# First batch of an attention and mixer kernel: token mixer by head pairs and column halves, one PSUM tile over four banks, reordered loads

## The chip, the cores and the metric

The kernel runs on one core of one Trainium2 chip. The metric is the device time of one execution in microseconds (us). Before the change the median was 291.68 us of three timed runs (291.28 to 292.91). Lower is better. Differences under 2% count as the same.

The engines are called PE (TensorE, matmuls), ACT (ScalarE), DVE (VectorE), POOL (GpSimd) and SP (SyncE, which issues stores). PSUM is the memory that PE's matmuls write and that ACT and DVE read here; the kernel divides it into eight banks of 512 fp32 columns.

## The reference, cut to what matters

```python
# 8 batches, 8 heads, 576 tokens, head size 64
scores = q @ k^T / 8 + min(-(cum_i - cum_j), 0), causal
attn   = exp(scores - max) / (sum + 1e-9)
x = (attn @ v) laid out as [batch, 576, 512]
h = relu(x^T @ w_tok1) @ w_tok2          # token mixer, 576 -> 256 -> 576
u = x + h^T
out = u + relu(u @ w_ch1) @ w_ch2        # channel mixer, 512 -> 1536 -> 512
```

## The kernel before

The kernel doesn't leave the order to a compiler. It lists operations with estimated durations, a small list scheduler (the plan) puts them in order on each engine, and the kernel then issues them in that order. A `Buf` is a claim on one slot of a ring of buffers. The plan gives it the slot that has been free longest.

All PSUM is in two rings: `psc`, two tiles of two banks each, for scores, and `pmx`, four tiles of one bank each, for nearly everything else:

```python
r_sc = ring("psc", 2, [128, 2, 512], FP32, psum)
r_mx = ring("pmx", 4, [128, 512], FP32, psum)
```

The groups of matmuls that write `pmx` are 316 in all (so many claims the plan makes on its slots): attention times v, token mixer and both channel matmuls of all eight batches. A group is written by PE and read by ACT or DVE, and with four slots PE can run up to three groups ahead of the readers. The tile framework adds the semaphores that keep a write and a read of the same tile apart.

The first channel matmul is the pattern that fills most of the time:

```python
pm = Buf(r_mx, False)
...
def mm(cc=cc, pm=pm, a=a, e=e):
    for m in range(NMC):          # 4 matmuls into one bank
        nc.tensor.matmul(out=pm.t[:, 0 : e - a], lhsT=wc1[:, m, bass.ds(cc * 128, 128)],
                         rhs=uT.t[:, m, a:e], start=(m == 0), stop=(m == NMC - 1))
...                               # then relu of that bank into g, on ACT or DVE
```

In batch one, scores of two head pairs go to two `pmx` slots (`Duo`) where `psc` is short. The causal mask is either a DVE multiplication behind the exponential, or, for the blocks in the list `FOLD`, matmuls that add -30000 to the scores (a "mask matmul" with the identity as weights):

```python
FOLD = ((0, 0), (0, 1), (1, 0), (1, 1), (2, 1), (3, 1))   # (head pair, group)
```

Where the plan sees PE idle in the first 95 us, the kernel puts matmuls on a zero tile there ("filler"), to keep PE's clock up.

## Time and profile before

| | span, profiled | PE busy | DVE | ACT | clock granted to PE |
|---|---|---|---|---|---|
| before | 294.8 us | 282.3 us (96%) | 192.9 us | 169.0 us | 0.981 |

The span is that of the profiled execution, which was a slow one (296.72 us; its clock fell to a half early on, as the prediction reads from it). Busy time counts an engine's instructions. The granted clock is the share of full speed at which PE could run, averaged over the span. The prediction below shows the lines behind this table.

### The profile page before, as it was taken

To read this page: it belongs to the slowest core of one execution; us is meant where nothing else is said; L and a number is where in the kernel's file an instruction comes from. 1 tells how busy PE (TensorE), PEld (TensorE's weight loads), DVE (VectorE), ACT (ScalarE), POOL (GpSimd) and SP (SyncE) were. 2 spreads that over 40 slices of the span, in tenths; PEclk is the share of its full clock that TensorE was granted. 3 is DMA by queue.
4 is the path that set the end of the run, shared out by engine and by line. 5 is a ranking of instruction groups with operands and counts; after the bars stand their busy time and mean duration, and the time that the engine had idled before them with its cause. 6 is when DMAs were issued, how large, how long until landed. Compare 5 with 4: busy or idle time off the path is not lost.

```text
span 294.8 us, 6480 instructions
## 1 busy us (share of the span) xinstructions
PE 282.3 (96%) x2565; PEld 161.9 (55%) x2597; DVE 192.9 (65%) x427; ACT 169.0 (57%) x286; POOL 45.3 (15%) x97
## 2 busy tenths in 40 slices
PE   7799999999999999999899999999999999999993
PEld 3348875656764554546664544536764454447642
DVE  7746947899998988999976687897236350530022
ACT  4365775989977858537781239672860346108500
POOL 8674600121111012102100022100000000000000
PEclk9759999999999999999999999999999999999999
DMA  7999999899674899857941786853002410250032
GB/s 134 222 203 263 216 209 218 183 235 272 95 141 92 116 235 204 163 118 191 170 69 37 143 167 107 123 120 115 0 3 54 129 69 0 58 140 36 3 107 76
DMA packets 58483, 38.60 MB, mean 131 GB/s; under 512 B 44496, under 2 KB 48208, under 8 KB 58448
## 3 DMA queue, kind: packets, MB, share of 16 engines
q0 software_dynamic: 10128, 17.93, 34.9%
q1 hardware_dynamic: 48320, 20.21, 28.4%
q8 instruction: 21, 0.34, 0.5%
q14 instruction: 14, 0.11, 0.1%
HBM read 40.71 MB, written 9.44 MB: 170 GB/s over the span
## 4 chain that ended last, share of the span: by engine, by line
PE 77%; DMA 5%; DVE 3%; issue 2%; ACT 2%; POOL 0%; POOLq 0%; ACTq 0%
PE pmx L979 30%; PE pmx L952 26%; PE psc L670 4%; PE pmx L813 4%; PE pmx L743 4%; PE pmx L883 4%; DMA qkn<-in_q_dram 3%; DMA qkn<-in_k_dram 2%; PE pmx L1098 1%; DVE x L753 1%; ACT junk L598 1%; PE psc L813 1%; DVE vp L570 1%; PE pmx L872 1%; ACT E L698 1%
## 5 line engine op out<-in xcount | busy, mean ns | idle before, releaser
L698 ACT ACTIVATE E<-psc 128x1024 bf16<-128x1024 f32 x62 | 60.3, 1021 | 41.9 <-PE psc L670 36.0
L952 PEld LDWEIGHTS <-wc 128*128 128x128 bf16 x624 | 59.7, 98 | 33.2 <-issue 2.3
L952 PE MATMUL pmx<-uTb,wc 128*128 128x320 bf16 x384 | 54.7, 299 | 1.0 <-ACT gb L959 1.0
L979 PE MATMUL pmx<-wc,gb 128*128 128x512 bf16 (+1 forms) x243 | 54.2, 369 | 0.6 <-issue 0.2
L959 ACT ACTIVATE gb<-pmx 128x320 bf16<-128x320 f32 x73 | 31.0, 440 | 27.2 <-PE pmx L952 22.7
L598 ACT ACTIVATE junk<-qkn 128x1152 bf16<-128x1152 bf16 x32 | 37.2, 1162 | 13.5 <-DMA qkn<-in_k_dram 8.0
L979 PE MATMUL pmx<-wc,ga 128*128 128x512 bf16 x182 | 44.1, 379 | 0.5
L952 PE MATMUL pmx<-uTa,wc 128*128 128x512 bf16 (+1 forms) x235 | 43.1, 336 | 0.4
L979 PEld LDWEIGHTS <-gb 128*128 128x128 bf16 x252 | 23.8, 98 | 24.9 <-issue 0.4
L959 ACT ACTIVATE ga<-pmx 128x512 bf16<-128x512 f32 (+1 forms) x48 | 23.7, 503 | 12.8 <-PE pmx L952 11.7
L706 DVE TENSOR_TENSOR E<-E,keep 128x512 bf16<-128x512 bf16 x58 | 23.9, 415 | 8.1 <-ACT E L698 7.4
L979 PEld LDWEIGHTS <-ga 128*128 128x128 bf16 x192 | 17.7, 98 | 19.7 <-issue 1.0
L753 DVE TENSOR_TENSOR x<-pmx,rc 128x320 bf16<-128x320 f32 x60 | 27.5, 481 | 0.7
L670 PE MATMUL psc<-qT,kT 32*128 32x256 bf16 (+2 forms) x620 | 24.3, 258 | 2.9 <-DVE qT L642 1.9
L570 DVE TENSOR_TENSOR vp<-vf,wT 128x512 bf16<-128x512 f32 (+1 forms) x40 | 26.1, 681 | 1.0 <-DMA vf<-in_v_dram 0.8
L743 PEld LDWEIGHTS <-E 128*128 128x128 bf16 x576 | 21.5, 97 | 6.4 <-issue 0.9
L670 PEld LDWEIGHTS <-kT 32*128 32x128 bf16 x640 | 15.3, 95 | 16.7 <-issue 14.4
L743 PE MATMUL pmx<-vp,E 128*128 128x65 bf16 x540 | 21.8, 193 | 0.0
L991 DVE TENSOR_TENSOR of<-pmx,ub 128x512 f32<-128x512 f32 (+1 forms) x17 | 11.2, 658 | 15.7 <-PE pmx L979 15.4
L642 DVE STREAM_TRANSPOSE qT<-qkn 128x576 f32<-128x576 f32 x16 | 19.9, 1241 | 2.3 <-DMA qkn<-in_q_dram 2.3
L991 DVE TENSOR_TENSOR of<-pmx,ua 128x512 f32<-128x512 f32 x12 | 8.3, 691 | 19.5 <-PE pmx L979 17.5
L592 POOL DMA_DIRECT2D qkn<-in_k_dram x20 | 10.8, 542 | 65.3 <-DVE E L714 36.9
(98 smaller groups left out, 245.5 us busy)
## 6 DMA issues: line engine op xcount, KB each, us to landing
out_dram<-of SPq DMA_DIRECT2D x31, 256.0 KB, 2.3
vf<-in_v_dram SPq DMA_DIRECT2D x24, 256.0 KB, 6.3
qkn<-in_k_dram POOLq DMA_DIRECT2D x20, 288.0 KB, 5.6
qkn<-in_q_dram POOLq DMA_DIRECT2D x20, 288.0 KB, 6.4
vf<-in_v_dram POOLq DMA_DIRECT2D x8, 256.0 KB, 9.1
wc<-in_moe_w_ch_dram POOLq DMA_DIRECT2D x4, 384.0 KB, 8.1
wc<-in_moe_w_ch_dram POOLq DMA_DIRECT2D x3, 512.0 KB, 11.5
out_dram<-of SPq DMA_DIRECT2D x10, 128.0 KB, 2.4
```

Source lines behind the costliest of these rows:

```text
L570: eng.tensor_tensor(out=vp.t[p0 : p0 + n, c, :, 0:D], in0=vf.t[p0 : p0 + n, c, :, :], in1=wT[p0 : p0 + n, cw, b * H : b * H + H].unsqueeze ...
L598: P.op({"ACT": (1.2, 1.6, lambda: nc.scalar.activation(out=junk[:, :], in_=n.t[:, :], func=AF.Square, accum_out=sq[:, col : col + 1]))}, r ...
L642: P.op({"DVE": (1.24, 1.4, lambda n=n, dst=dst: nc.vector.transpose(out=dst.t[:, 0:S, :].rearrange("d t e -> d (t e)").bitcast(FP32).rearr ...
L670: nc.tensor.matmul(out=pss[g // 2].bank(g % 2)[:, o], lhsT=kT.t[rows, j0 : j0 + 128, e], rhs=qT.t[rows, a:z, e], start=(e == 0 and not (fo ...
L698: nc.scalar.activation(out=E.t[:, :, gi * 512 : gi * 512 + 512], in_=ps.t[:, :, :], func=AF.Exp, scale=0.125)
L706: nc.vector.tensor_tensor(out=o, in0=o, in1=keep[:, :].unsqueeze(1).unsqueeze(1).to_broadcast([128, 2, 2, 128]), op=ALU.mult)
L743: nc.tensor.matmul(out=o[:, i, ic, 0 : D + 1], lhsT=E.t[:, hh, d0 : d0 + 128], rhs=vp.t[:, jc, h + hh, 0 : D + 1], start=(jc == j_lo), sto ...
L753: nc.vector.tensor_tensor(out=x.t[:, :, h0 * D : (h0 + n) * D].rearrange("p c (e d) -> p e c d", e=n), in0=view()[:, :, :, 0:D], in1=rc.t[ ...
L952: nc.tensor.matmul(out=pm.t[:, 0 : e - a], lhsT=wc1[:, m, bass.ds(cc * 128, 128)], rhs=uT.t[:, m, a:e], start=(m == 0), stop=(m == NMC - 1))
L959: lambda cc=cc, pm=pm, a=a, e=e: nc.scalar.activation(out=g.t[:, cc, a:e], in_=pm.t[:, 0 : e - a], func=AF.Relu),
L979: nc.tensor.matmul(out=pm.t[:, 0 : d1 - d0], lhsT=g.t[:, cc, c * 128 : c * 128 + 128], rhs=wc2[:, cc, d0:d1], start=(cc == 0), stop=(cc == ...
L991: nc.vector.tensor_tensor(out=o.t[:, d0:d1], in0=pm.t[:, 0 : d1 - d0], in1=src.t[:, si, d0:d1], op=ALU.add)
```

## The change

The intent is to shorten the way from the first scores to the first channel matmul, and to close holes in PE's order behind it. The core of the diff, cut:

```diff
-    LAG = 3.0
+    LAG = 2.5
-    FOLD = ((0, 0), (0, 1), (1, 0), (1, 1), (2, 1), (3, 1))
+    FOLD = ((0, 1), (1, 0), (1, 1), (2, 0), (2, 1), (3, 0), (3, 1))
...
-    r_mx = ring("pmx", 4, [128, 512], FP32, psum)
+    banks = psum.tile([128, 4, 512], FP32, name="pmx", tag="pmx")
+    r_mx = Ring("pmx", [banks[:, i, :] for i in range(4)])
...  (class Duo: two slots are now one access over two banks)
+        def t(self):
+            lo, hi = sorted(x.slot for x in self.bufs)
+            return banks[:, lo : hi + 1 : hi - lo, :]
...  (pads: memsets on DVE become copies of a zero tile on ACT)
...  (normalisation: by pairs, the third pair as ten copies with a scale on ACT)
-        for hs in ([(0, 1)] if b == 0 and np_ > 1 else [(0,), (1,)]):
+        for hs in ([(0, 1)] if b == 0 else [(0,), (1,)]):
...  (token mixer of batch one: four cuts of two heads, second matmul by column halves)
-        cuts = [[(0, 4)], [(4, 6)], [(6, H)]] if b == 0 else ...
+        cuts = [[(0, 2)], [(2, 4)], [(4, 6)], [(6, H)]] if b == 0 else ...
...  (loads of batch two: keys earlier, second half of the first channel weight later,
...   first part of the second channel weight ahead of the last query; estimates of three loads)
-                 ...], ("wc2", g), 3.1)
+                 ...], ("wc2", g), 2.6)
...  (some of the last stores split in two; a fallback that doesn't run loads through POOL)
```

More of the change, by code (lines that the diff above doesn't have):

```diff
@@ L238, in general @@
             tc.tile_pool(name="genp", bufs=1, space=bass.MemoryType.PSUM) as pp:
-        nc.sync.dma_start(out=scr[:, :], in_=cum[:, :])
+        nc.gpsimd.dma_start(out=scr[:, :], in_=cum[:, :])
         past = gp.tile([128, 1152], FP32, name="gk", tag="gk")
@@ L251, in general @@
                     sl = src[bass.ds(b, 1), bass.ds(h, 1), :, :]
-                    nc.sync.dma_start(out=f[:, 0:4, :],
+                    nc.gpsimd.dma_start(out=f[:, 0:4, :],
                                       in_=sl[:, :, 0:512, :].rearrange("o u (c p) d -> p (o u c) d", p=128))
-                    nc.sync.dma_start(out=f[0:64, 4, :], in_=sl[:, :, 512:576, :].rearrange("o u p d -> (o u p) d"))
+                    nc.gpsimd.dma_start(out=f[0:64, 4, :], in_=sl[:, :, 512:576, :].rearrange("o u p d -> (o u p) d"))
                     n = g2.tile([128, NJ, D], BF16, name="gn", tag=f"gn{len(nat)}")
@@ L267, in general @@
                 nc.vector.memset(cb[:, S:640], 0.0)
-                nc.sync.dma_start(out=cb[:, 0:S], in_=scr[bass.ds(b * H + h, 1), :].to_broadcast([128, S]))
+                nc.gpsimd.dma_start(out=cb[:, 0:S], in_=scr[bass.ds(b * H + h, 1), :].to_broadcast([128, S]))
                 with tc.For_i(0, NJ, 1) as ic:
@@ L339, in general @@
                 nc.vector.tensor_tensor(out=o[:, :], in0=pm[0:64, :], in1=o[:, :], op=ALU.add)
-                nc.sync.dma_start(out=out[bass.ds(b, 1), bass.ds(c * 64, 64), :].rearrange("o p d -> (o p) d"), in_=o[:, :])
+                nc.gpsimd.dma_start(out=out[bass.ds(b, 1), bass.ds(c * 64, 64), :].rearrange("o p d -> (o p) d"), in_=o[:, :])
 @with_exitstack
@@ L478, in late_pads, with ones, tok_pads, v_pads @@
     def late_pads():
-        for i in range(2, 4):
-            P.op({"DVE": (0.15, 0.3, lambda i=i: pads(nc.vector, i)), "POOL": (0.4, 0.6, lambda i=i: pads(nc.gpsimd, i))},
-                 reads=["wT"], writes=[("pad", i)], prio=40)
-        P.op({"DVE": (0.6, 0.8, lambda: pads2(nc.vector)), "POOL": (1.0, 1.2, lambda: pads2(nc.gpsimd))},
-             reads=["wT"], writes=["padw"], prio=41)
-        P.op({"DVE": (0.3, 0.5, lambda: pads3(nc.vector, 1)), "POOL": (0.5, 0.7, lambda: pads3(nc.gpsimd, 1))},
-             reads=["wT"], writes=["padv"], prio=42)
+        def ones(i):
+            nc.scalar.activation(out=r_E.tiles[i][:, :, EW - 64 : EW], in_=zero[:, 0:128].rearrange("p (h n) -> p h n", h=2),
+                                 func=AF.Copy, bias=1.0, scale=1.0)
+        def tok_pads():
+            nc.scalar.copy(out=w1[64:128, NJ - 1, :], in_=zero[64:128, 0:DT])
+            nc.scalar.copy(out=w1[0:64, NJ, :], in_=zero[0:64, 0:DT])
+            nc.scalar.copy(out=w2[:, :, S : NJ * 128], in_=zero[:, 0 : NTC * 64].rearrange("p (t n) -> p t n", t=NTC))
+        def v_pads():
+            for h in range(0, H, 4):
+                nc.scalar.copy(out=r_vp[1].tiles[0][0:64, NJ - 1, h : h + 4, :],
+                               in_=zero[0:64, 0 : 4 * (D + 2)].rearrange("p (h n) -> p h n", h=4))
+        for i in range(2, 4):
+            P.op({"ACT": (0.3, 0.5, lambda i=i: ones(i))}, writes=[("pad", i)], prio=40)
+        P.op({"ACT": (0.9, 1.1, tok_pads)}, writes=["padw"], prio=41)
+        P.op({"ACT": (0.7, 0.9, v_pads)}, writes=["padv"], prio=42)
     s_sb = sb("s_sb", [64, S], FP32, fast)
@@ L545 @@
     vbuf = {}
+    later = []
     gate = sb("gate", [1, 32], BF16, fast)
@@ L561, in stage_v @@
             else:
-                load_p(load, [(vf, c)], (0.75 if b or c <= 1 else 1.25) * n / 128, 1.4)
+                load_p(load, [(vf, c)], (0.75 if b or c == 0 else 1.3) * n / 128, 1.4)
                 yield
@@ L572, in mul @@
                     in1=wT[p0 : p0 + n, cw, b * H : b * H + H].unsqueeze(2).to_broadcast([n, H, D]), op=ALU.mult)
-            P.op({"DVE": (0.72, 0.95, lambda mul=mul: mul(nc.vector))}, reads=[(vf, c), "wT"], writes=[(vp, c)], prio=b * 10 + 5 if b else 0)
+            o = P.op({"DVE": (0.72, 0.95, lambda mul=mul: mul(nc.vector))}, reads=[(vf, c), "wT"], writes=[(vp, c)], prio=b * 10 + 5 if b else 0)
+            if b == 1:
+                later.append(o)
         def ones():
@@ L593, in load_quad @@
             out=n.t[:, :], in_=src[b, 4 * qd : 4 * qd + 4, :, :].rearrange("g (p r) d -> (g p) (r d)", r=R)),
-            [(n, 0)], 128 * 0.19 / 16)
+            [(n, 0)], 128 * 0.182 / 16)
         return n
@@ L620, in __init__ @@
             self.keys = [(x, 0) for x in self.bufs]
+        @property
+        def t(self):
+            lo, hi = sorted(x.slot for x in self.bufs)
+            return banks[:, lo : hi + 1 : hi - lo, :]
         def bank(self, g):
-            return self.bufs[g].t[:, :]
+            return self.t[:, g, :]
     class Solo:
@@ L677, in quad @@
                     fold = (np_ + e, gi) in FOLD
-                    occ = 0.8 + 0.4 * gi if fold else 0.58
+                    occ = 0.6 + 0.1 * gi if fold else 0.55
                     P.op({"PE": (occ, occ + 0.3, lambda e=e, mm=mm, fold=fold: mm((2 * e, 2 * e + 1), fold))},
@@ L691, in soft @@
         odd = b % 2
-        def ex2():
-            for g in range(2):
-                nc.scalar.activation(out=E.t[:, g, gi * 512 : gi * 512 + 512], in_=ps.bank(g), func=AF.Exp, scale=0.125)
         def ex():
             nc.scalar.activation(out=E.t[:, :, gi * 512 : gi * 512 + 512], in_=ps.t[:, :, :], func=AF.Exp, scale=0.125)
-        P.op({"ACT": (1.18, 1.4, ex2)} if isinstance(ps, Duo) else act(1024, ex), reads=ps.keys, writes=[(E, jc) for (jc, a, z) in group], prio=0)
+        P.op(act(1024, ex), reads=ps.keys, writes=[(E, jc) for (jc, a, z) in group], prio=0)
         if b == 0 and (np_, gi) in FOLD:
@@ L726, in pair @@
         vkeys = [(vp, c) for c in range(NJ)] + [(vp, "w")] + (["padv"] if b == 1 else [])
-        for hs in ([(0, 1)] if b == 0 and np_ > 1 else [(0,), (1,)]):
-            pa = Solo(r_sc if b == 0 and np_ > 1 else r_mx)
+        for hs in ([(0, 1)] if b == 0 else [(0,), (1,)]):
+            pa = Duo() if b == 0 and np_ < 2 else Solo(r_sc if b == 0 else r_mx)
             rc = Buf(r_rc, False)
@@ L755, in nrm, with nrm_act @@
                     in1=rc.t[:, 0:n, :].unsqueeze(3).to_broadcast([128, n, NJ, D]), op=ALU.mult)
-            P.op({"DVE": (0.16 + 0.33 * n, 0.38 + 0.33 * n, nrm)}, reads=pa.keys + [(rc, 0)], writes=[(x, h + hh) for hh in hs], prio=0)
+            def nrm_act(view=view, rc=rc, h0=h + hs[0]):
+                for i in range(2):
+                    for c in range(NJ):
+                        nc.scalar.activation(out=x.t[:, c, (h0 + i) * D : (h0 + i + 1) * D], in_=view()[:, i, c, 0:D],
+                                             func=AF.Copy, scale=rc.t[:, i, c : c + 1])
+            P.op({"ACT": (1.5, 1.72, nrm_act)} if np_ == 2 else {"DVE": (0.16 + 0.33 * n, 0.38 + 0.33 * n, nrm)}, reads=pa.keys + [(rc, 0)], writes=[(x, h + hh) for hh in hs], prio=0)
     def load_w(dmas, key, us):
@@ L779, in load_ch2 @@
         load_w([(wc2[:, 4 * g : 4 * g + 4, :],
-                 moe_w_ch2[g * 512 : (g + 1) * 512, :].rearrange("(c p) n -> p c n", p=128))], ("wc2", g), 3.1)
+                 moe_w_ch2[g * 512 : (g + 1) * 512, :].rearrange("(c p) n -> p c n", p=128))], ("wc2", g), 2.6)
     hbuf = {}
@@ L796, in tok @@
         us = Buf(r_us) if odd else None
-        cuts = [[(0, 4)], [(4, 6)], [(6, H)]] if b == 0 else [[(0, 4)], [(4, H)]] if b == 1 else [[(0, H)]]
+        cuts = [[(0, 2)], [(2, 4)], [(4, 6)], [(6, H)]] if b == 0 else [[(0, 4)], [(4, H)]] if b == 1 else [[(0, H)]]
         for part in cuts:
             h0, h9 = part[0][0], part[-1][1]
-            late = h0 > 0
+            late = h0 >= 4
             if late:
@@ L834, in tok, with mmT @@
                 hk = [(h1, t, part[0][0]) for part in cuts if part[0][0] <= 2 * m < part[-1][1] for t in range(NTC)]
-                def mmT(m=m, pm=pm):
-                    o = slice(m * 128, m * 128 + 128)
-                    for t in range(NTC):
-                        nc.tensor.matmul(out=pm.t[:, :], lhsT=h1.t[:, t, o], rhs=w2[:, t, 0:NQ], start=(t == 0), stop=False)
-                    for c in range(NJ - 1):
-                        nc.tensor.matmul(out=pm.t[:, c * 128 : c * 128 + 128], lhsT=x.t[:, c, o], rhs=ident[:, :],
-                                         start=False, stop=(c == NJ - 2))
-                occ = 2 * c_pe(NQ)[0] + 4 * c_pe(128)[0]
-                P.op({"PE": (occ, occ + 0.3, mmT)}, reads=hk + ["w2", (x, 2 * m), (x, 2 * m + 1)],
-                     writes=[(pm, 0)], holds=[uT], prio=(rank - TOK, 1 + 0.1 * m))
-                for a in (0, NQ // 2):
+                for a in (0, NQ // 2):
+                    def mmT(m=m, pm=pm, a=a):
+                        o = slice(m * 128, m * 128 + 128)
+                        for t in range(NTC):
+                            nc.tensor.matmul(out=pm.t[:, a : a + NQ // 2], lhsT=h1.t[:, t, o], rhs=w2[:, t, a : a + NQ // 2],
+                                             start=(t == 0), stop=False)
+                        for c in range(a // 128, a // 128 + 2):
+                            nc.tensor.matmul(out=pm.t[:, c * 128 : c * 128 + 128], lhsT=x.t[:, c, o], rhs=ident[:, :],
+                                             start=False, stop=(c == a // 128 + 1))
+                    occ = 2 * c_pe(NQ // 2)[0] + 2 * c_pe(128)[0]
+                    P.op({"PE": (occ, occ + 0.3, mmT)}, reads=hk + ["w2", (x, 2 * m), (x, 2 * m + 1)],
+                         writes=[(pm, a)], holds=[uT], prio=(rank - TOK, 1 + 0.1 * m + (0.25 if a else 0)))
                     def evT(eng, m=m, pm=pm, a=a):
@@ L852, in evT @@
                             nc.vector.tensor_copy(out=o, in_=i)
-                    P.op(either(NQ // 2, lambda evT=evT: evT(0), lambda evT=evT: evT(1)), reads=[(pm, 0)],
-                         writes=[(uT, m, a)], prio=0)
+                    o = P.op(either(NQ // 2, lambda evT=evT: evT(0), lambda evT=evT: evT(1)), reads=[(pm, a)],
+                             writes=[(uT, m, a)], prio=0)
+            for w in later:
+                w.deps.add(o)
         hkeys = [(h1, t, part[0][0]) for part in cuts for t in range(NTC)]
@@ L1000, in st @@
                     if c < NJ - 1:
-                        nc.sync.dma_start(out=out[b, c * 128 : c * 128 + 128, d0:d1], in_=o.t[:, d0:d1])
+                        parts = 2 if (b == B - 1 and c < 3) or (b == B - 2 and c == 3) else 1
+                        for i in range(parts):
+                            w = (d1 - d0) // parts
+                            f0 = d0 + i * w
+                            nc.sync.dma_start(out=out[b, c * 128 : c * 128 + 128, f0 : f0 + w], in_=o.t[:, f0 : f0 + w])
                     else:
@@ L1020 @@
     load_tok()
+    sv = stage_v(1)
     load_ch1(0, 0)
     load_ch1(0, 1)
-    sv = stage_v(1)
-    for m2 in range(2):
-        next(sv)
-        load_ch1(1, m2)
-    for i in range(2):
-        next(sv)
-        stage_qk(1, 0, (i,))
-    run(sv)
-    stage_qk(1, 1)
-    for g in range(3):
-        load_ch2(g)
+    next(sv)
+    load_ch1(1, 0)
+    next(sv)
+    stage_qk(1, 0, (0,))
+    next(sv)
+    load_ch1(1, 1)
+    stage_qk(1, 0, (1,))
+    next(sv)
+    next(sv)
+    run(sv)
+    stage_qk(1, 1, (0,))
+    load_ch2(0)
+    stage_qk(1, 1, (1,))
+    load_ch2(1)
+    load_ch2(2)
     last[0] = P.op({"SP": (0.6, 0, lambda: nc.sync.dma_start(out=gate[0:1, 16:32], in_=wc2[0:1, NCC - 1, 0:16]))},
```

## The prediction

> **What bounds the kernel now.** I read the page's busy shares and its 40 slices first, then sums over chosen stretches, then the timeline of TensorE (PE), then that of VectorE (DVE) where PE waited, then the waits and the landings of the weight loads.
>
> ```profile
> PE 282.3 (96%) x2565; PEld 161.9 (55%) x2597; DVE 192.9 (65%) x427; ACT 169.0 (57%) x286; POOL 45.3 (15%) x97
> ...
> PEclk9759999999999999999999999999999999999999
> DMA  7999999899674899857941786853002410250032
> ```
>
> PE is busy 96% of a span of 294.8 us; no other engine passes 65%. Adding up its idle time, I find 1.3 us at the start, 0.6 and 1.9 us before the first scores, 1.0 us near 147, 0.5 us near 194 and 4.6 us behind the last matmul (a store and the closing of the program). The rest are crumbs. So the kernel is bound by PE, and a change gains only where PE is idle, slow, or busy with nothing. The second line says slow: the granted clock falls to about a half in slices 2 and 3.
>
> ```profile
> core 0: us, PE busy (x) PEld busy (x) DVE busy (x) ACT busy (x) POOL busy (x), PEclk, DMA share, GB/s
> 10.80:21.00 10.20, 9.84 (x82) 4.27 (x81) 6.47 (x13) 6.43 (x9) 7.59 (x11) 0.50 1.17 198
> 40.20:44.40 4.20, 4.15 (x47) 2.67 (x48) 3.28 (x7) 3.21 (x4) 0.28 (x1) 1.00 1.17 212
> ```
>
> From 10.8 to 21.0 us, which is the scores of the first batch, PE had half its clock: 10.2 x 0.5 = 5.1 us of capacity lost. The DMA share is above 1: the loads of batches one and two and of all weights fill the queues from about 5 to 54 us. The profiled execution took 296.72 us, the timed ones 291.28 to 292.91; the 5.0 us between 296.72 and the median of 291.68 is about this loss. I conclude (it isn't shown) that the timed runs mostly keep the clock in this stage.
>
> "Busy with nothing" is line 1098: matmuls on a zero tile that the schedule puts wherever it believes PE idle, to hold the clock. They count as busy but are holes of the plan. In the timeline of PE (start, length, line, operation, count, idle time before):
>
> ```profile
> 10.29 0.40 PE L670 MATMUL psc<-qT,kT 32*128 32x256 bf16 x4 [1.89 <-DVE qT L642]
> ...
> 23.56 0.55 PE L1098 MATMUL pmx<-zero 128*128 128x512 bf16 x2
> ...
> 24.70 0.25 PE L1098 MATMUL pmx<-zero 128*128 128x205 bf16 x1
> ...
> 29.62 0.81 PE L1098 MATMUL pmx<-zero 128*128 128x512 bf16 x3
> 30.26 0.60 PE L952 MATMUL pmx<-uTa,wc 128*128 128x256 bf16 x4
> ...
> 41.42 1.10 PE L1098 MATMUL pmx<-zero 128*128 128x512 bf16 x4
> 42.45 0.64 PE L670 MATMUL psc<-qT,kT 32*128 32x256 bf16 x24
> 43.02 1.36 PE L1098 MATMUL pmx<-zero 128*128 128x512 bf16 x6
> 44.21 1.89 PE L979 MATMUL pmx<-wc,ga 128*128 128x512 bf16 x8
> ```
>
> Two holes matter. **Hole A**, in the token mixer of batch one: 0.43 us (23.56), 0.24 us (24.70) and 0.65 us (29.62 to 30.3, counting the part that doesn't overlap), about 1.3 us. **Hole B**, ahead of the second channel matmul: from the last L952 at 41.58 to L979 at 44.38 on the chain is 2.80 us with one real piece of 0.57 us in it, so 2.2 us.
>
> What makes hole A is VectorE:
>
> ```profile
> 22.64 0.49 DVE L753 TENSOR_TENSOR x<-pmx,rc 128x320 bf16<-128x320 f32 x1
> ...
> 23.32 1.25 DVE L753 TENSOR_TENSOR x<-pmx,rc 128x320 bf16<-128x320 f32 x3
> 24.49 0.47 DVE L749 RECIPROCAL rc<-psc 128x10 f32<-128x10 f32 x2
> 24.88 1.49 DVE L753 TENSOR_TENSOR x<-psc,rc 128x640 bf16<-128x640 f32 x2
> ```
>
> Normalisation holds DVE from 22.41 to 26.37 without a break, and the first token matmul (24.79) takes four heads at once, so it waits until 24.57, while PE had finished those heads' attention at 23.2. What makes hole B isn't a semaphore: the list of waits has none for PE there. The three loads of the second channel weight were issued at 28.70, 29.54 and 30.88. The first and the last took:
>
> ```profile
> DMA to landing us min/median/max: 9.8/9.8/9.8
> ...
> DMA to landing us min/median/max: 13.8/13.8/13.8
> ```
>
> They landed at 38.5, 41.0 and 44.7, but the plan charges 3.1 us each and so expects them later. In the profiled run hole B was in the plan's estimates more than in the data. The lines of waits have one more thing:
>
> ```profile
> DVE uTa L852 <- ACT uTa L850: 2.4, 3, 1.3
> ```
>
> The two halves of one evacuated bank go to ScalarE and VectorE, and the second engine waits for the first.
>
> **What the Trainium skill says.** "TensorE: Matmul & The Clock Gate", Part 1: the array's clock is halved after a window of some 3.4 us with little activity and restored after a busy one, and the windows run free of the kernel. The trace agrees: 10.2 us at 0.50, three such windows, behind an idle 1.89 us. "PSUM — Partial Sum Buffer", PSUM bank collisions: two engines must be kept apart on one bank. The 2.4 us above is that separation. "VectorE: DVE Perf Modes", Why PSUM operands drop a tier: fp32 from PSUM stays at the base rate, so pairing saves only fixed cost. The trace agrees: 320 columns take 0.48 us, 640 take 1.49/2 = 0.75 us.
>
> **The change part by part.**
>
> Pads to ScalarE: takes two E pads (0.31 us at 10.20), three weight pads (0.45 us) and one v pad (0.28 us) from DVE, 1.04 us. ScalarE was idle from 7.52 to 11.81. Only the 0.31 us stands between two transposes, and the last query lands at 12.54, hence little: 0 to 0.2 us.
>
> Masks: one block of masks leaves PE (pair 0, first group), two come (pairs 2 and 3). A block is four matmuls of 128 columns, 0.05 us each at full clock: +0.2 us of PE, +0.4 at half. The first exponential starts 0.2 to 0.4 us earlier in return. Net 0.
>
> Exponentials over joined banks: two of 512 took 1.09 us, one of 1024 takes 1.02; two places, -0.14 us.
>
> Normalisation: before, DVE took 4 x 0.48 + 4 x 0.16 + 1.49 + 0.47 = 4.5 us by single durations (4.0 us in the timeline, where they overlap). After, three pairs at about 0.95 are 2.9 us, and the fourth pair is ten copies of 64 columns on ScalarE. Its 128-column relu pairs took 0.45 us, 0.22 each, so ten are 1.3 to 2 us (estimate), beside DVE. DVE is free about 1.1 us earlier.
>
> Token mixer by pairs and halves: the same columns on PE (the first two cuts become 20 x 0.056 in place of 10 x 0.108), but the first cut starts after one pair, and the first-half channel matmuls can start while PE still has second halves to do. This fills hole A: I count 1.1 of its 1.3 us.
>
> Loads and estimates: the first second-channel load passes one 288 KB query load, 1.39 us by the landings (34.52 to 35.91), so it lands near 37.1. The estimate falls from 3.1 to 2.6 us, close to the measured 2.55. The filler of hole B should go, but the third load still lands near 44, so some waiting comes back: I count 1.5 of 2.2 us.
>
> The later order (LAG 2.5), the delayed multiplication of v of batch two and the split stores: no sure sign, 0. The last store's chain, issue at 290.67 and landing at 292.85, isn't shortened. The fallback's loads don't run.
>
> Sum: 0.1 + 0.1 + 1.1 + 1.5 = 2.8 us. With a little more for the lower LAG, chosen rather than derived, 3.1 us: 291.7 - 3.1 = 288.6.
>
> **The rivals.** (1) The loads take hole B's place. In a run at full clock PE is up to 5 us earlier, near 36.5 at the end of L952, where the first weight load (37.1) and above all the third (44) bind. For it: DMA share 1.17. Against: scores and attention of batch two are there to fill. Time 290.5. (2) VectorE becomes the bound in batches two and three, where it is busy 9.19 of 10 us (50 to 60) and 18.73 of 20 (60 to 80), and returns the gain. For it: those shares. Against: PE never waits on it there. Time 290 to 291. (3) One joined tile for four banks makes waits between unrelated banks, or ScalarE's ten copies delay the relus behind them: 291.5 to 293. The trace of before can't tell. (4) Both holes close wholly and the warmer PE keeps its clock in more runs: 3.7 us, perhaps 5, thus 286.5 to 288.
>
> **Range and chances.** The gain I can point to is at most 3.7 us of holes plus small change, 1.3%; over 2% (under 285.85) needs a clock effect on top: 0.10. Slower by 2% (above 297.5) needs rival 3 at its worst: 0.02. The range 286.2 to 291.2 spans rivals 1, 2 and 4.
>
> **What would show it.** Right: L952 starts a good microsecond earlier at equal clock; filler between 23 and 30 us and between L952 and L979 nearly gone; DVE's normalisation near 3 us; the first second-channel load landing ahead of a query; the PE timeline behind 60 us shifted, not changed. Wrong: new PE waits on second-channel loads or on DVE between 36 and 60 us; more idle PE behind 100 us than the 1.0 and 0.5; a clock at half for longer or shorter than 10.2 us, which alone moves the time by 1.7 us a window.

## More of the kernel before

One more line, to be held against the changed kernel later, is the sum over 100 us in the steady part (columns: stretch, its length, busy time of PE, weight loads, DVE, ACT and POOL with instruction counts, clock, DMA share, GB/s):

```profile
100.00:200.00 100.00, 97.57 (x918) 52.30 (x928) 83.30 (x186) 61.01 (x96) 11.19 (x29) 1.00 0.72 142
```

PE works 97.6 of 100 us, at full clock.

## The result, and the profile after

The changed kernel took 569.36 us (median of four runs, 565.47 to 574.37) against 291.48 us of the kernel before in the same rounds. The ratio is 1.948, with a 95% interval of 1.931 to 1.966. Ratios here and below are the mean time of one kernel's fast runs over that of the other's of the same rounds, so not quite the ratio of the medians. The output is correct. The profiled run is a fast one; the slow run (574.37 us) counts in the median of four but not in the ratio.

The page of the changed kernel, the lines that answer to those of before:

```profile
span 570.2 us, 6541 instructions
...
PE 376.5 (66%) x2589; PEld 182.9 (32%) x2620; DVE 196.4 (34%) x413; ACT 175.5 (31%) x305; POOL 44.8 (8%) x97
...
PEclk9975997985789999995579979686579999788579
```

No engine is the bound any more. DVE and ACT have nearly the work of before (DVE 196.4 against 192.9 us, ACT 175.5 against 169.0) and PE has the same instructions within 1%, yet PE is busy for 376.5 instead of 282.3 us and idle for 193.7 instead of 12.5 us. Of the 275.4 us by which the span grew, 181.2 us are PE idle and 94.2 us are PE busy for longer. The clock is not lost once, at the start, but again and again over the whole span (mean 0.841). Weighing each busy stretch of PE with the clock granted in it, 66.0 us of its busy time are lost to the clock, against 4.9 us before (an estimate from the two traces). The rest of the 94.2 us is paid at full clock: the four matmuls of the group at 33.60 us, alone but at full clock, took 0.60 us, against the 0.44 us that such four take back to back.

The profile of before is a slow one. Between the fast profiles of the two controls below the split is the same: the span grows by 277.6 us, of which 180.9 us are PE idle and 96.7 us PE busy for longer.

The sums over a stretch early and over the same 100 us as before (same columns):

```profile
40.00:60.00 20.00, 13.91 (x60) 7.34 (x60) 0.00 (x0) 4.60 (x12) 0.00 (x0) 0.62 0.78 153
100.00:200.00 100.00, 62.46 (x518) 31.63 (x523) 46.31 (x101) 36.53 (x58) 6.94 (x21) 0.86 0.39 76
```

From 40 to 60 us all that the compute engines do is 60 matmuls, their weight loads and 12 ACT instructions. Between 100 and 200 us PE issues 518 matmuls instead of 918. This is long behind the first batch, for which the change was written.

What such a stretch is made of is seen in the timelines of PE and ACT (start, length, line, operation, count, idle time before and what ended it):

```profile
39.10 1.01 PE L977 MATMUL pmx<-uTa,wc 128*128 128x256 bf16 x4 [0.47 <-ACT ga L984]
40.59 1.01 PE L977 MATMUL pmx<-uTa,wc 128*128 128x256 bf16 x4 [0.47 <-ACT ga L984]
```

```profile
38.67 0.38 ACT L984 ACTIVATE ga<-pmx 128x256 bf16<-128x256 f32 x1 [1.10 <-PE pmx L977]
40.15 0.38 ACT L984 ACTIVATE ga<-pmx 128x256 bf16<-128x256 f32 x1 [1.10 <-PE pmx L977]
```

The two engines take turns. PE writes a group (39.10 to 40.11), ACT reads (40.15 to 40.53), PE writes the next (from 40.59), with a period of 1.49 us. In the kernel before, the same four matmuls took 0.44 us each time (84 of them in 9.17 us on the chain), and the readers ran beside them. Inside a group the matmuls start 0.21 us apart in place of 0.11: this is half clock (0.50 granted from 39.0 to 41.1 us). The Trainium skill, "TensorE: Matmul & The Clock Gate", A second HAM failure mode: psum-queue depth-cycling, describes PE idling briefly and often between groups until the clock swings between its two states. This trace agrees: 0.47 us idle in each 1.49, and a clock of 0.62 from 40 to 60 us.

The waits of the whole span, the lines that matter (who waited for whom: total us, times, longest):

```profile
ACT gb L984 <- PE pmx L977: 97.8, 55, 25.7
...
PE pmx L977 <- ACT gb L984: 33.1, 55, 1.1
...
PE pmx L977 <- ACT ga L984: 23.0, 33, 1.9
```

The list of before has a single wait of PE for ACT at that line, of 1.0 us. The waits of 33.1 and 23.0 us are the largest that joined the list; waits of PE for DVE, up to 11.4 us in all at a line, joined it too.

With the changed kernel in hand I read the semaphores in the compiled programs, which needs no chip. A group of the first channel matmul in the changed kernel, with the counts that it waits for and reaches:

```
PE   4 matmuls into bank 2   first waits for ACT count 101 (a read of bank 0); last makes PE count 786
ACT  read of bank 1          waits for PE count 786 (the write of bank 2);     makes ACT count 102
PE   4 matmuls into bank 3   first waits for ACT count 102 (the read of bank 1)
```

Every line here waits for another bank than its own. Here each access waits for the last access by another engine to the tile, whatever bank that touched. In the kernel before each bank is a tile, so the same rule makes a group wait for the reader of its own bank, four groups ago. I counted over each program the PE waits whose releaser touches PSUM:

```
                        reader of the same bank   reader of another bank, same tile
kernel before                    305                          3
changed kernel                    31                        277
```

A second count, which puts the wait of a weight load down to the matmul behind it, gave 307 and 1, and 34 and 274.

This makes a theory: the one tile over four banks costs everything (theory A). Three rivals stand against it. In B, the new plan's order, the copies on ACT or the loads lose the time. In C, an instruction that reads two banks is slow. In the third, the loss comes from the banks and their ports, and sharing a tile is incidental.

### The profile page after: what moved, and what is told of

It reads as the page before. It is cut to its first block, busy times and chain, and to the rows that moved or that the text cites. A ratio compares the mean times of both kernels' runs of the same rounds, so it can differ in the third digit from the quotient of the medians.

```text
span 570.2 us, 6541 instructions
## 1 busy us (share of the span) xinstructions
PE 376.5 (66%) x2589; PEld 182.9 (32%) x2620; DVE 196.4 (34%) x413; ACT 175.5 (31%) x305; POOL 44.8 (8%) x97
## 4 chain that ended last, share of the span: by engine, by line
PE 61%; DVE 18%; ACT 12%; issue 6%; DMA 2%; another core or an unknown queue 1%; POOL 0%; DVEq 0%; ACTq 0%; POOLq 0%
PE pmx L977 26%; PE pmx L1004 19%; ACT gb L984 6%; DVE x L768 5%; ACT ga L984 4%; PE pmx L758 4%; DVE of L1016 4%; PE pmx L834 4%; PE pmx L908 2%; DVE gb L986 2%; PE psc L689 2%; DVE rc L764 1%; DVE ub L930 1%; DVE ua L930 1%; DVE ga L986 1%
## 5 line engine op out<-in xcount | busy, mean ns | idle before, releaser
L977 PE MATMUL pmx<-uTb,wc 128*128 128x320 bf16 x384 | 90.4, 379 | 51.1 <-ACT gb L984 33.1
L977 PEld LDWEIGHTS <-wc 128*128 128x128 bf16 x624 | 70.4, 113 | 155.8 <-issue 118.3
L1004 PE MATMUL pmx<-wc,gb 128*128 128x512 bf16 (+1 forms) x243 | 65.1, 405 | 28.3 <-DVE of L1016 7.3
L977 PE MATMUL pmx<-uTa,wc 128*128 128x512 bf16 (+1 forms) x234 | 58.0, 381 | 33.9 <-ACT ga L984 23.0
L1004 PE MATMUL pmx<-wc,ga 128*128 128x512 bf16 x182 | 54.2, 431 | 22.2 <-DVE ub L930 5.1
L768 DVE TENSOR_TENSOR x<-pmx,rc 128x320 bf16<-128x320 f32 (+1 forms) x58 | 28.3, 496 | 30.1 <-PE pmx L1004 8.4
L612 ACT ACTIVATE junk<-qkn 128x1152 bf16<-128x1152 bf16 x32 | 37.1, 1160 | 2.3 <-DMA qkn<-in_k_dram 2.0
L986 DVE TENSOR_SCALAR gb<-pmx 128x320 bf16<-128x320 f32 x21 | 10.3, 491 | 58.3 <-PE pmx L977 40.6
L834 PE MATMUL pmx<-x,w 128*128 128x512 bf16 (+2 forms) x88 | 21.1, 372 | 12.3 <-DVE x L768 4.2
L908 PE MATMUL pmx<-h,w 128*128 128x512 bf16 x55 | 16.2, 387 | 10.9 <-DVE of L1016 4.1
L689 PE MATMUL psc<-qT,kT 32*128 32x256 bf16 (+1 forms) x620 | 22.7, 258 | 0.7
```

What stands on the lines that cost most here:

```text
L612: P.op({"ACT": (1.2, 1.6, lambda: nc.scalar.activation(out=junk[:, :], in_=n.t[:, :], func=AF.Square, accum_out=sq[:, col : col + 1]))}, r ...
L689: nc.tensor.matmul(out=pss[g // 2].bank(g % 2)[:, o], lhsT=kT.t[rows, j0 : j0 + 128, e], rhs=qT.t[rows, a:z, e], start=(e == 0 and not (fo ...
L768: nc.vector.tensor_tensor(out=x.t[:, :, h0 * D : (h0 + n) * D].rearrange("p c (e d) -> p e c d", e=n), in0=view()[:, :, :, 0:D], in1=rc.t[ ...
L834: nc.tensor.matmul(out=pm()[:, (ha - h0) * D : (hb - h0) * D], lhsT=w1[:, NJ if odd and c == NJ - 1 else c, t * 128 : t * 128 + 128], rhs= ...
L908: nc.tensor.matmul(out=pm.t[:, :], lhsT=w2[:, t, c * 128 : c * 128 + 128], rhs=h1.t[:, t, :], start=(t == 0), stop=(t == NTC - 1 and not f ...
L986: lambda cc=cc, pm=pm, a=a, e=e: nc.vector.tensor_scalar_max(out=g.t[:, cc, a:e], in0=pm.t[:, 0 : e - a], scalar1=0.0)),
```

## The experiments

All kernels below leave out the conditional fallback block behind the main part, which never runs with these inputs; it contains a form of weight load that these experiments had to avoid. So two controls come first. The twelve runs gave correct outputs. They were timed in three groups, each on a chip of its own and beside the kernel before (c1, c2, e1, e2; e3 to e6; e7 to e10). Across groups the ratios to the kernel before are compared, rather than the medians.

### The two controls

> Control: the kernel before without the conditional fallback block, which never runs with these inputs (the experiments all leave it out). Every theory: the time of before less at most 1 us of closing, 290 to 292 us; ratio to before 0.995 to 1.00.

> Control: the changed kernel without the fallback block. Every theory: about the time of the changed kernel, 560 to 575 us. If the moved fallback loads were to blame, it would fall to about 290 us; I don't expect that.

The control of before took 290.61 us, ratio 0.995 (0.988 to 1.002). The control of after took 568.06 and 577.05 us, the second slow. The fallback isn't involved.

The control of before had its profile in the fast state (clock 0.998, span 288.7 us), which before's own profile had not. So its timeline shows what the prediction could only infer:

```profile
13.41 0.29 PE L670 MATMUL psc<-qT,kT 32*128 32x256 bf16 x2
...
14.09 0.59 PE L660 MATMUL psc<-negm,ident 128*128 128x512 bf16 x2
...
17.28 1.02 PE L743 MATMUL pmx<-vp,E 128*128 128x65 bf16 x28 [0.48 <-DVE vp L570]
...
25.47 9.33 PE L952 MATMUL pmx<-uTa,wc 128*128 128x256 bf16 x84
...
38.23 1.36 PE L1098 MATMUL pmx<-zero 128*128 128x512 bf16 x6
39.42 1.89 PE L979 MATMUL pmx<-wc,ga 128*128 128x512 bf16 x8
```

The first channel matmul starts at 25.47 us here and the second at 39.42, with filler ahead of it. Both are 4.8 us earlier than in the profile at half clock. The first three lines are for later: from 13.41 to 14.09 us PE does 16 score matmuls, of two head pairs at once, and at 17.28 us attention times v goes on after a wait for v.

### Only the joined tile undone, and only the joined tile done

```diff
 # e1, against the changed kernel
-    banks = psum.tile([128, 4, 512], FP32, name="pmx", tag="pmx")
-    r_mx = Ring("pmx", [banks[:, i, :] for i in range(4)])
+    r_mx = ring("pmx", 4, [128, 512], FP32, psum)
 # and two instructions, one for each bank, where one read both
```

```diff
 # e2, against the kernel before: nothing else
-    r_mx = ring("pmx", 4, [128, 512], FP32, psum)
+    banks = psum.tile([128, 4, 512], FP32, name="pmx", tag="pmx")
+    r_mx = Ring("pmx", [banks[:, i, :] for i in range(4)])
```

> The changed kernel with only the joined PSUM tile undone: four separate one-bank tiles, two instructions where one read two banks. Theory A (the one tile over four banks makes each matmul group wait for the read of another bank): the whole loss goes, 286 to 291 us, and the blind sum of the other parts (288.6 us, less the 0.1 us of the joined exponentials) gets its test. Rival B (the order and the delays of the new plan, or ScalarE's copies, lose the time): stays above 400 us. Mixed: between.

> The kernel before with only the joined PSUM tile: one tile of four banks, each ring slot a slice of it, every instruction, order and shape as before. Theory A: 550 to 580 us, PE waits on ScalarE and VectorE for over 100 us, clock near 0.85. Rival B: about 291 us. Rival C (reading two banks in one instruction is what is slow): about 291 us too, as nothing here reads two banks.

The changed kernel with four tiles took 291.37 us, ratio 0.998 (0.990 to 1.006). The kernel before with one tile took 581.84 us, ratio 1.993 (1.975 to 2.010). Its page:

```profile
PE 391.4 (67%) x2566; PEld 186.0 (32%) x2597; DVE 199.8 (34%) x427; ACT 170.2 (29%) x286; POOL 45.2 (8%) x97
...
PEclk9955697999798899975797597575779959885569
```

The longest wait in its list of waits of PE is the changed kernel's:

```profile
PE pmx L953 <- ACT gb L960: 30.3, 51, 1.2
```

The waits that this list shows for ACT and DVE add up to over 120 us. Both times lie just outside what theory A expected (291 and 580 us at most), and the clock is 0.799 in place of some 0.85. The record's own class for e2 is "unclear" (it has two runs), but an interval of 1.975 to 2.010 leaves the loss in no doubt.

That one change of the tile, with every instruction, shape and order as before, gives the whole loss and the swinging clock. Undoing it takes the whole loss away. Theory A stands, B and C fall. The joined exponentials and normalisations themselves, which read two banks, aren't in e2 at all.

### Two tiles of two banks, dealt out in two ways

```diff
 # e3 (neighbours share): tile i // 2, bank i % 2.   e4 (alternate): tile i % 2, bank i // 2
+    pairs = [psum.tile([128, 2, 512], FP32, name=f"pmx{i}", tag=f"pmx{i}") for i in range(2)]
+    r_mx = Ring("pmx", [pairs[i // 2][:, i % 2, :] for i in range(4)])
```

> The kernel before with two tiles of two banks in place of four of one; ring slots 0 and 1 share a tile, 2 and 3 the other. Theory A (a group waits for the last reader of its tile, whichever bank that read): where slots follow each other in turn, every second group waits for the read of the group just before it, about half of the loss of the joined kernel: 400 to 460 us. Rival (only one tile over all banks is bad, or the loss comes from the banks themselves): as fast as before, 291 us, or as slow as the joined one.

> The same two tiles of two banks, only dealt out differently: slots 0 and 2 share a tile, 1 and 3 the other. Theory A: the read that a group waits for is that of the group before last, and runs beside the last group's matmuls; a group is 0.54 to 0.86 us at full clock, a read 0.4 to 0.6 us[...], so the waits are short: 295 to 360 us, well below the neighbouring deal. Rival (size or number of tiles counts, not the order): the same time as with neighbours sharing.

They took 339.93 us (ratio 1.162, 1.155 to 1.169) and 332.44 us (1.136, 1.129 to 1.144). The page of the first:

```profile
PE 291.7 (86%) x2566; PEld 161.9 (48%) x2597; DVE 195.7 (58%) x427; ACT 165.9 (49%) x286; POOL 45.2 (13%) x97
```

The direction is theory A's: fewer banks on a tile, less loss, and the alternating deal is a little faster. The size of the effect of the deal was wrong: I expected 400 to 460 against 295 to 360, and measured 340 against 332. The programs tell why. The plan takes whatever slot has been free longest, so the slots don't follow in turn, and both deals mix. Counting how many groups back the data lies whose read a group waits for:

```
                   waits counted   at most 2 groups back
four tiles              287                  8
one tile                266                208
two tiles, e3           200                109
two tiles, e4           191                 76
```

A second count, with the plan's claims on slots as the groups, gave 15, 219, 118 and 81: other numbers in the same order. The time follows that last column. It also follows the clock: with two tiles PE is busy 86% and keeps 0.998 of its clock, with one tile 67% and 0.799. That the one tile costs some 290 us and two tiles only 40 to 50 fits this: with one tile the waits also bring down the clock. No run separates the two, but e2's trace gives an estimate. Its span is 292.0 us longer than the control's (580.7 against 288.7). Of that, 179.3 us are PE idle. PE's busy time grew by 112.7 us (391.4 less the control's 278.7): 85.9 us are lost to the clock, weighed as above, and 26.8 us are paid at full clock. In e3, which kept its clock, PE's busy time grew by 13.0 us.

The banks and ports as such are the same four in all of e1 to e4, and only the grouping into tiles differs. The third rival falls too.

### Where the expected 2.8 us went

e1 is the changed kernel as it was meant, and it isn't faster than the control. Its timeline of PE:

```profile
9.62 0.63 PE L683 MATMUL psc<-qT,kT 32*128 32x256 bf16 x8 [1.41 <-DVE qT L655]
...
14.46 0.40 PE L683 MATMUL psc<-qT,kT 32*128 32x256 bf16 x4
14.79 0.29 PE L673 MATMUL psc<-negm,ident 128*128 128x128 bf16 x2
15.01 0.40 PE L683 MATMUL psc<-qT,kT 32*128 32x256 bf16 x4
...
16.56 0.59 PE L673 MATMUL psc<-negm,ident 128*128 128x512 bf16 x2
...
32.44 2.75 PE L1145 MATMUL pmx<-zero 128*128 128x512 bf16 x11
35.02 3.22 PE L990 MATMUL pmx<-uTa,wc 128*128 128x256 bf16 x28
```

Two things stand out. The 16 score matmuls of pairs 2 and 3 that took 0.68 us in the control (13.41 to 14.09) take 2.10 us here (14.46 to 16.56), since mask matmuls stand between them. And the hole ahead of the second channel matmul is gone, but 11 zero matmuls stand in the middle of the first one, where the plan waits for the weight's second half. Two kernels take these apart:

```diff
 # e5, against e1: load order and load estimates as before
 # e6, against e1:
-    FOLD = ((0, 1), (1, 0), (1, 1), (2, 0), (2, 1), (3, 0), (3, 1))
+    FOLD = ((0, 0), (0, 1), (1, 0), (1, 1), (2, 1), (3, 1))
 # (and the estimates that belong to it)
```

> Four separate tiles, and the change without its new load order and load estimates. In the split kernel the hole ahead of the second channel matmul is gone, but 11 zero matmuls (2.6 us) stand in the middle of the first channel matmul. If the new order and estimates moved that hole: here the middle hole goes, a hole ahead of the second channel matmul comes back with about 2 us, and the time stays within 1 us of the split kernel (290.4 to 292.4). If they were a gain in themselves: 2 us slower than the split kernel.

> Four separate tiles, the change with the old list of masked blocks. In the split kernel the second half of the first batch's scores takes 2.2 us on TensorE for the blocks of pairs 2 and 3, before 0.7 us, because mask matmuls stand between score matmuls that used to run two pairs at once, and ScalarE idles 1.4 us. If that is where the token mixer's gain went: the first channel matmul starts 1.0 to 1.7 us earlier than the split kernel's 27.2 us and the time is 0.5 to 1.5 us below it. If the delay comes from ScalarE's ten copies (2.15 us): no change.

e5 took 291.29 us (0.996, 0.992 to 1.001), the same as e1. Its middle hole is gone, and 18 zero matmuls stand ahead of the second channel matmul, more than the 2 us I expected. e6 took **288.01 us** (0.985, 0.980 to 0.990), 3.4 us less than e1, more than the 0.5 to 1.5 us that I expected, and the fastest of all. Against the kernel before it is 1.5% faster, which counts as the same, and of that 0.5% is the left-out fallback by the control's ratio (whose interval, 0.988 to 1.002, just overlaps e6's). Its first channel matmul starts 2.5 us earlier than e1's:

```profile
17.14 1.02 PE L761 MATMUL pmx<-vp,E 128*128 128x65 bf16 x28 [0.71 <-DVE vp L581]
...
24.69 5.40 PE L990 MATMUL pmx<-uTa,wc 128*128 128x256 bf16 x48
29.93 2.30 PE L1145 MATMUL pmx<-zero 128*128 128x512 bf16 x9
```

Not all of the 2.5 us is the mask blocks'. In e1's profile the first query landed later and the first score matmul starts at 9.62 us, in e6's at 8.41 us; among all these profiles this start lies anywhere from 8.39 to 9.65 us in kernels at full clock. From the first score matmul to the first channel matmul e1 takes 17.57 us (e5 17.47) and e6 16.28: 1.3 us less, as expected. How much of the 3.4 us of time is the mask blocks' and how much such landings isn't separated.

So the new list of mask blocks was itself a loss. The Trainium skill, "TensorEngine Tiling (Array Packing)", Key Properties, says that tiles of the array work in parallel, and that a change of the tiling mode drains PE. Score matmuls use 32 rows each and mask matmuls all 128. The trace agrees. Of the 1.42 us, the eight mask matmuls account for 8 x 0.054 = 0.43 us. The scores now start two at a time in eight steps, where the control starts four at a time in four steps, of 0.12 us each: 0.46 us of lost overlap. The other 0.5 us lies at the changes between the two kinds, six more than in the control, about 0.09 us each (an estimate by subtraction). The lines show it: the two mask matmuls at 14.79 us have 0.11 us of columns, and the next score starts 0.22 us after the first of them.

The last four runs vary the faster kernel, and the kernel before:

```diff
 # e7, against e6: third pair normalised on DVE, no copies on ACT
 # e8, against e6: second half of wc1 loaded ahead of batch two's first key
 # e9, against the kernel before: only the new load order and load estimates
 # e10, against e6:
-    LAG = 2.5
+    LAG = 3.0
```

> The faster kernel so far (four separate tiles, old list of masked blocks) with the third pair's normalisation back on VectorE: one instruction of about 0.8 us in place of ten copies that took 2.15 us on ScalarE. If the copies hold up the token mixer (TensorE waits 0.40 us for them at 21.3 us): first channel matmul 0.3 to 1.0 us earlier than 24.7 us, time 287.0 to 288.0. If VectorE's queue was the bound, as the blind prediction had it: 0.5 to 1 us later.

> The faster kernel so far with the second half of the first channel weight loaded ahead of batch two's first key. If the hole in the middle of the first channel matmul (9 zero matmuls, 2.1 us) is the plan's waiting for that load: the middle hole goes. Whether the time follows: rival 1 of the prediction (the loads as a whole bind) says the hole comes back ahead of the second channel matmul and the time stays within 0.7 us of 288.0; otherwise 286.0 to 287.0.

> The kernel before with only the new load order and the new load estimates. The blind prediction gave this part 1.5 us: 289.1 us. Rival 1 (loads bind, the hole moves): 290 to 291.5 us, with as many zero matmuls behind 20 us as before (13), at other places.

> The faster kernel so far with the old lag of 3.0 in place of 2.5. The blind prediction put some 0.3 us on the lower lag without deriving it. If the lag makes part of the 2.6 us by which this kernel beats the control: 288.5 to 290; if not: 287.5 to 288.5.

e7 took 288.18 us (0.991, 0.986 to 0.997): no difference from e6 that these runs resolve. The first channel matmul started at 25.44 us, 0.75 us later than in e6 as the prediction's view of DVE has it. But 0.43 us of that is there already where attention times v goes on after its wait for v (17.57 against 17.14 us), so some 0.3 us is left for the normalisation, and the end of the kernel didn't follow.

e8 took 289.79 us (0.995, 0.992 to 0.998). The first channel matmul now runs through, and 11 zero matmuls come behind it:

```profile
25.17 10.64 PE L990 MATMUL pmx<-uTa,wc 128*128 128x256 bf16 x96
36.31 2.42 PE L1145 MATMUL pmx<-zero 128*128 128x512 bf16 x11
```

The hole moved, and the time rose by 1.8 us, which neither theory had. The profile puts most of it later: six more zero matmuls from 57.5 us on (1.3 us) and waits of PE of 0.43 us (at 56.4 us) and 0.41 us (at 122.8 us), none of which e6 has.

e9 took 289.71 us (0.994, 0.991 to 0.998). The control's ratio is 0.995, so no gain in time is resolved. Here the filler behind 20 us fell from 13 to 4 matmuls, against what I expected of rival 1, and the second channel matmul starts at 37.44 us, 2.0 us earlier than in the control. But later it waits 0.85 us for a transposed tile (at 131.5 us) and 1.50 us for ACT (at 169.6 us); the control's two largest waits in its second hundred microseconds are 1.20 and 0.34 us. From the list of waits of PE in e9:

```profile
PE pmx L952 <- ACT ga L959: 1.5, 1, 1.5
```

In the profiles, 1.3 of the 2.0 us gained are given back behind the start of the second channel matmul: from there to the last matmul e9 takes 247.2 us and the control 245.9.

e10 took 288.77 us (0.992, 0.988 to 0.996), within what I expected if the lag makes part of the gain. But its interval and that of e6 overlap, so the lag's share stays open. The profiles give a hint: with the lag of 3.0, e10 waits 0.98 us for ACT at 168.8 us, at the place where e9 waits 1.50 us, and e6, e7 and e8 with 2.5 don't wait there.

## Why the prediction was right or wrong

It was wrong by 281 us, and the failed step is rival 3: "One joined tile for four banks makes waits between unrelated banks". The mechanism was named, but its size was not worked out: the sum has no term for it, its time was put at 291.5 to 293 us (at most 1.3 us above 291.68), the range leaves it out, and a loss of over 2% got a chance of 0.02, since "The trace of before can't tell". The runs showed a loss of 291 us from the joined tile alone (e2, 581.84 against the control's 290.61), of which 179.3 us are PE idle and 85.9 us are lost to the clock.

One thing should have warned, and one reading would have told. The warning is the scope. The title speaks of the first batch, but the joined tile is the ring of all 316 groups, so any wait that it adds can be paid by every group of the kernel. At the 0.47 us of idle time per group that the changed kernel's trace shows, that alone is some 150 us (an estimate, and only possible afterwards). The reading is the tile of two banks that the kernel before already had, `psc`. A pair of relus reads its two banks separately in the token mixer:

```profile
27.85 0.45 ACT L826 ACTIVATE h<-psc 128x128 bf16<-128x128 f32 x2 [0.19 <-PE psc L813]
```

PE wrote that tile's first bank with the first five of ten matmuls (27.09 to 27.81 us for all ten, the fifth ending at 27.54), and ACT was free from 27.66, but the first relu began only after the tenth. In the program it waits for the last write to the second bank. The rule was there to be seen, at a place where it cost next to nothing.

The other steps:

- **PE bounds the kernel before, and the timed runs keep the clock.** Right, and now shown: the control's profile has a clock of 0.998 and starts the first channel matmul at 25.47 us, 4.8 us earlier than the half-clock profile. Of the 25 runs of the kernel before that were timed beside the experiments, 20 had a clock of 0.996 or more.
- **Masks, "Net 0".** Wrong. The term was mis-sized because I charged the mask matmuls their own columns only. They also break the overlap of the score matmuls and add changes between the two kinds: 1.42 us on PE in the second half of the scores. The gain in return was there: the first exponential starts 0.67 us after the first score matmul in e1, 1.21 us in the control. The first channel matmul still came 1.3 us later than with the old list (e1 against e6, from the first score matmul on).
- **Normalisation.** The ten copies on ACT were estimated at 1.3 to 2 us and took 2.15 us. A joined pair on DVE took 0.82 us plus 0.22 for the reciprocal, against 0.95 estimated. e7 shows no effect on the time from where the third pair is normalised.
- **Token mixer, 1.1 us of hole A.** Right in place, about twice too large: with the old mask list the first channel matmul starts 0.8 us before the control's (24.69 against 25.47), and counted from where attention times v goes on after its wait for v, 0.6 us (7.55 against 8.19 us).
- **Loads and estimates, 1.5 us of hole B.** Right in place in e9: the first second-channel load was to land near 37.1 and landed at 37.1 (issue at 27.24 us and 9.9 us), and the second channel matmul came 2.0 us earlier. Wrong in the end: no gain in time that the runs resolve. In e1 and e6 the hole moved into the first channel matmul (rival 1), in e9 waits came later.
- **Three readings of the lines that don't hold as put.** The "measured 2.55" us of a second-channel load is the step between the first two landings; the next step was 3.7 us (41.0 to 44.7), and the mean is the 3.1 us that the plan charged. "The 2.4 us above" is all the time that DVE idled in front of the three reads; ACT's reads before them took 0.37 us each, so at most 1.1 us is the separation of the two engines. And PE counts as busy for 9.84 of the 10.2 us at half clock, yet the clock didn't come back after the first of the three windows, as it should have by the prediction's account of a busy window; why, stays open.
- **"With a little more for the lower LAG".** Open.
- **The sum.** Without the joined tile and with the old mask list the change gives 288.01 us, near the predicted 288.6. That is luck in part, as the terms above differ.

What stays open is what the joined tile's waits alone would cost at full clock. By the estimate above it is some 206 of the 292 us, if the waits kept their lengths; no run had the one tile and the full clock.

## What to carry to other kernels

Before several buffers become slices of one tile, ask what unit the program's semaphores guard, and count how many groups use the ring: joining buffers for one instruction's convenience can take away the double buffering of the whole kernel. Such a join could be kept to a tile used only where it's needed (not tried here). And when small matmuls run side by side on parts of the array, a full-array matmul placed between them costs more than its columns.

## What the Trainium skill lacked or had wrong

- "PSUM — Partial Sum Buffer" tells to guard by bank and quadrant. It doesn't say that a program's own guards may be coarser than a bank when several banks are one tile: one tile over four banks took 581.84 us where four tiles took 290.61, two tiles of two banks 332 to 340 us.
- "TensorE: Matmul & The Clock Gate" has the two clock states and the swinging between them, but no share of busy time at which a kernel of short waits falls into it. Here 86% busy kept 0.998 of the clock, and 67% busy had 0.799.
- "TensorEngine Tiling (Array Packing)" names the parallel tiles and the drain on a change of mode, without a cost. Here 16 score matmuls of 32 rows took 0.68 us, and 2.10 us with eight mask matmuls over the full array between them; about 0.09 us of that is paid at each change (an estimate).
